# A three-operation gelu derivative, eight evictions on VectorE, and a later fill in the last chunk of a speech joint's gradients

## The chip, the core and the metric

The kernel runs on one core of a Trainium2 chip. A core has five engines that work side by side, each through its own queue of instructions in order: TensorE (PE; its weight loads are listed as PEld), VectorE (DVE), ScalarE (ACT), GpSimd (POOL) and SyncE (SP, which only issues DMAs here). The metric is the time of one execution on the device in microseconds, and the figure is the median of several runs.

## The reference

The reference is a forward pass with its gradients. Two batches of 16000 rows with 256 features go through two convolutions of three taps, each followed by the tanh form of gelu and by dropping every second row, which leaves 4000 rows. Their projection is added to that of eight prompt rows, tanh is taken of every pair, and a last product gives the output. All seven gradients are returned with it.

```python
def _fwd_reference(x, w1, w2, g, w_f, w_g, w_o):
    ...
    for i in range(K):
        h = h + jnp.einsum("btc,cd->btd", xp[:, i:i+T, :], w1[i])
    h = _gelu(h)[:, ::2, :]
    ...
    for i in range(K):
        f = f + jnp.einsum("btc,cd->btd", hp[:, i:i+T1, :], w2[i])
    f = _gelu(f)[:, ::2, :]
    fe = jnp.einsum("btd,de->bte", f, w_f)
    ge = jnp.einsum("bud,de->bue", g, w_g)
    j = jnp.tanh(fe[:, :, None, :] + ge[:, None, :, :])
    return jnp.einsum("btud,dv->btuv", j, w_o)

def reference(x, w1, w2, g, w_f, w_g, w_o, grad_out):
    ...
    _out, _vjp = jax.vjp(_f, x, w1, w2, g, w_f, w_g, w_o)
    _grads = _vjp(grad_out)
```

## The kernel before

The 2 x 4000 columns that remain lie in one row of 8016 (16 columns between the batches are padding). It is cut into 16 chunks of 512; the last has 336. An iteration n of the main loop (L865) does the joint of chunk n, four pairs of prompt rows after each other (`joint_units`, L705), and beside it, as a "fill" that `weave` (L773) deals out in steps between the joint's own steps, the forward convolutions of chunk n+1 (`conv_units`, `conv2_units`, `fe_units`) and the backward pass of chunk n-1 (`d1_units` to `e_units`). A framework fixes each engine's instruction order when the program is built. It follows the written order, its own estimate of when inputs are ready, and some orders that the kernel demands (`add_manual_dep`, `pinned`).

**Joint.** For each prompt row u, `tanh` (L423, ScalarE) writes JT and the square of it (L664, ScalarE) writes JSQ, which has two buffers. L672 (TensorE) multiplies the output gradient into a PSUM tile, and L676 (VectorE) makes NGZ of it and JSQ; there are two such tiles, mt = 0 and 1, for each u. GpSimd adds NGZ over the eight u into ACCN (L695); the last addition writes NGFE, which the backward product L460 reads. L721 (TensorE) makes the output in blocks of 128 columns, L723 (ScalarE) evicts each into OUT, and L748 stores it. L760 (TensorE) accumulates the gradient of w_o from JR, the transposed JT that SyncE fetches by a DMA transpose (L702).

**gelu.** `gelu` (L287) returns two lists of operations. The first (square, L277 product, sigmoid, second product) gives the activation. The second (L302 to L306) gives the derivative for the backward pass, with five VectorE operations. A chunk has three calls: two for the first convolution (its even and odd positions, G1) and one for the second (G2). The first lists run from a queue `later`, the second lists from a queue `late`, which is emptied in the second half of an iteration; from chunk 2 on their order is kept as written. In the profile the first list stands under L277, the line that takes it off its queue (or under L345); the second stands under L285 (the wrapper `pinned`) for chunks 2 to 15 and under L282 for chunks 0 and 1. G2 is read in L462, G1 in L486, and both multiply a PSUM tile.

**PSUM.** All products except the accumulator of L760 write to tiles of one pool of seven buffers (`psp`, L124), which are handed out in turn. Whoever asks for the eighth tile waits until the first has been emptied.

**Ends.** Iteration 0 has no backward pass; its fill starts with six empty steps. Iteration 15 has no forward pass. The fill that is left when the joint of an iteration has ended is done behind it (L899).

Of the kernel before, what the change touches and what calls it, by code (L numbers as in the profile page):

```python
# [15 lines left out]
ALU = mybir.AluOpType  # L16
# [2 lines left out]
GELU_K = 0.044715  # L19
GELU_R = float(np.sqrt(0.044715))  # L20
GELU_A = float(2.0 * np.sqrt(2.0 / np.pi))

P = 128
KT = 2
# [3 lines left out]
U = 8  # L28
CW = 512
# [3 lines left out]
def kernel(  # L33
# [250 lines left out]
    def pinned(op, n):  # L284
        return op if n <= 1 else (lambda: tc.keep_in_program_order(op()))  # L285

    def gelu(xb, W, h, gp, off, kts=((0, KT),), spare=False):  # L287

        sq, s = scratch("g_sq", spare), scratch("g_s", spare)
        TT, TS, STT = nc.vector.tensor_tensor, nc.vector.tensor_scalar, nc.vector.scalar_tensor_tensor  # L290
        first, second = [], []
        for (k0, k1) in kts:
            sq_, s_, x_ = sq[:, k0:k1, :W], s[:, k0:k1, :W], xb[:, k0:k1, :W]
            h_, gp_ = h[:, k0:k1, off:off + W], gp[:, k0:k1, off:off + W]
            first += [
                partial(nc.scalar.activation, out=sq_, in_=x_, func=ACT.Square, scale=GELU_R),
                partial(STT, out=s_, in0=sq_, scalar=1.0, in1=x_, op0=ALU.add, op1=ALU.mult),
                partial(nc.scalar.activation, out=s_, in_=s_, func=ACT.Sigmoid, scale=GELU_A),
                partial(TT, out=h_, in0=s_, in1=x_, op=ALU.mult),
            ]  # L300
            second += [
                partial(TS, out=sq_, in0=sq_, scalar1=3.0 * GELU_A, scalar2=GELU_A, op0=ALU.mult, op1=ALU.add),  # L302
                partial(TS, out=x_, in0=s_, scalar1=-1.0, scalar2=1.0, op0=ALU.mult, op1=ALU.add),
                partial(TT, out=sq_, in0=sq_, in1=x_, op=ALU.mult),
                partial(TT, out=sq_, in0=sq_, in1=h_, op=ALU.mult),
                partial(TT, out=gp_, in0=sq_, in1=s_, op=ALU.add),  # L306
            ]
        return first, second
# [2 lines left out]
    HALVES = ((0, 1), (1, 2))  # L311

    seconds0 = []

    def conv_units(n):
        c0, W = geom(n)
        seconds = []
        st = S[n]
        HT = htp.tile([P, 2, KT, CW + 2], BF16, name="HT")
        G1 = g1p.tile([P, 2, KT, CW + 2], BF16, name="G1")  # L320
        st["HT"], st["G1"] = HT, G1
        if n == G - 1:
            nc.gpsimd.memset(G1[:, 0, :, 2 + W:3 + W], 0.0)
        if n == 0:
            nc.gpsimd.memset(HT[:, 1, :, 1:2], 0.0)
            nc.gpsimd.memset(G1[:, 1, :, 1:2], 0.0)
        else:
            nc.gpsimd.tensor_copy(out=HT[:, 1, :, 1:2], in_=S[n - 1]["HT"][:, 1, :, CW + 1:CW + 2])
        taps = {0: ((1, 0, 0), (2, 1, 0), (0, 3, -1)), 1: ((0, 1, 0), (2, 3, 0), (1, 2, 0))}
        for par in range(2):  # L330
            xb = gel.tile([P, KT, CW], BF16, name="g_x")
            for mt in range(KT):
                ps = ps_f32()
                k = 0
                for (i, c, sh) in taps[par]:
                    for kt in range(KT):
                        nc.tensor.matmul(ps[:, :W], lhsT=W1[:, i, kt, mt * P:(mt + 1) * P],  # L337
                                         rhs=st["X", c][:, kt, 16 + sh:16 + sh + W], start=(k == 0), stop=(k == 5))
                        k += 1
                nc.scalar.copy(out=xb[:, mt, :W], in_=ps[:, :W])  # L340
                yield
            first, second = gelu(xb, W, HT[:, par], G1[:, par], 2, HALVES if n == 0 else ((0, KT),))
            if par == 1 and n > 1:
                for j in (1, 3):
                    first[j] = partial(lambda f: held.append(f()), first[j])  # L345
            later.extend(first)
            seconds += second
            if n == 0:
                pump(len(first))
        seconds0.extend(seconds)  # L350
        if n > 0:
            seconds0.append(lambda: nc.gpsimd.tensor_copy(out=G1[:, 1, :, 1:2],
                                                          in_=S[n - 1]["G1"][:, 1, :, CW + 1:CW + 2]))

    def conv2_units(n):
        c0, W = geom(n)
        st = S[n]
        HT = st["HT"]
        if n > 0:
            pump(len(later))  # L360
        FT = packed(ftp.tile([P, KT, CW], BF16, name="FT")[:], "k w", n, k=KT)
        G2 = ftp.tile([P, KT, CW], BF16, name="G2")
        st["FT"], st["G2"] = FT, G2
        xb = scratch("g_x", n == 0)
        for mt in range(KT):
            ps = ps_f32()
            k = 0
            for (i, par, off) in ((1, 0, 2), (0, 1, 1), (2, 1, 2)):
                for kt in range(KT):
                    nc.tensor.matmul(ps[:, :W], lhsT=W2[:, i, kt, mt * P:(mt + 1) * P],  # L370
                                     rhs=HT[:, par, kt, off:off + W], start=(k == 0), stop=(k == 5))
                    k += 1
            nc.scalar.copy(out=xb[:, mt, :W], in_=ps[:, :W])
            yield
        first, second = gelu(xb, W, FT, G2, 0, HALVES if n == 0 else ((0, KT),), n == 0)
        if n == 0:
            for f in first:
                f()
        else:
            later.extend(first)  # L380
        late.extend(pinned(f, n) for f in second + seconds0)
        seconds0.clear()
        late_open[0] = True
# [62 lines left out]
    def d1_units(n):  # L446
        c0, W = geom(n)
        st = S[n]
        GF = gfp.tile([P, KT, CW + 4], BF16, name="GF")
        st["GF"] = GF  # L450
        if n > 0:
            nc.gpsimd.tensor_copy(out=GF[:, :, 1:2], in_=S[n - 1]["GF"][:, :, CW + 1:CW + 2])
        else:
            nc.gpsimd.memset(GF[:, :, 1:2], 0.0)
        if n == G - 1:
            nc.gpsimd.memset(GF[:, :, 2 + W:3 + W], 0.0)
        for mt in range(KT):
            ps = ps_f32()
            for kt in range(KT):
                nc.tensor.matmul(ps[:, :W], lhsT=WFT[:, kt, mt * P:(mt + 1) * P], rhs=st["NGFE"][:, kt, :W],  # L460
                                 start=(kt == 0), stop=(kt == KT - 1))
            nc.vector.scalar_tensor_tensor(out=GF[:, mt, 2:2 + W], in0=st["G2"][:, mt, :W], scalar=-1.0,  # L462
                                           in1=ps[:, :W], op0=ALU.mult, op1=ALU.mult)
            yield

    def d5_units(n):
        st = S[n]
        c0, W = geom(n)
        N = W + 1 if n == G - 1 else W
        GF, G1 = st["GF"], st["G1"]  # L470
        GH = ghp.tile([P, 2, KT, CW + 4], BF16, name="GH")
        st["GH"] = GH
        if n == 0:
            nc.gpsimd.memset(GH[:, 0, :, 1:2], 0.0)
        else:
            nc.gpsimd.tensor_copy(out=GH[:, 0, :, 1:2], in_=S[n - 1]["GH"][:, 0, :, CW + 1:CW + 2])
        for par, taps in ((0, ((1, 0),)), (1, ((2, -1), (0, 0)))):
            for mt in range(KT):
                ps = ps_f32()
                k, last = 0, len(taps) * KT - 1  # L480
                for (i, sh) in taps:
                    for kt in range(KT):
                        nc.tensor.matmul(ps[:, :N], lhsT=W2T[:, i, kt, mt * P:(mt + 1) * P],  # L483
                                         rhs=GF[:, kt, 2 + sh:2 + sh + N], start=(k == 0), stop=(k == last))
                        k += 1
                gh = nc.vector.tensor_tensor(out=GH[:, par, mt, 2:2 + N], in0=ps[:, :N],  # L486
                                             in1=G1[:, par, mt, 2 - par:2 - par + N], op=ALU.mult)
                while held:
                    tc.add_manual_dep(held.pop().ins, gh.ins.name, NOSYNC, reason="held")
                yield  # L490
# [190 lines left out]
    def ngfe_acc(n, u):  # L681
# [10 lines left out]
        if u == U - 1:  # L692
            st["NGFE"] = ngp.tile([P, KT, CW], BF16, name="NGFE")
            out = st["NGFE"][:, :, :W]
        st["last"] = nc.gpsimd.tensor_tensor(out=out, in0=in0, in1=st["NGZ", u][:, :, :W], op=ALU.add)  # L695

    def load_jr(n, up):

# [6 lines left out]
    def joint_units(n, up):  # L705
# [10 lines left out]
        def o_block(k):  # L716
            o, M = bl[k]
            ps = ps_f32()
            for j, u in enumerate(us):
                for kt in range(KT):  # L720
                    nc.tensor.matmul(ps[:M, j * V:(j + 1) * V], lhsT=st["JT", u][:, kt, o:o + M], rhs=WO[:, kt, :],  # L721
                                     start=(kt == 0), stop=(kt == KT - 1))
            nc.scalar.copy(out=OUT[:M, k, :], in_=ps[:M, :])  # L723

        pend = prev_gwo[0]
        o_block(0)
# [138 lines left out]
    for n in range(G):  # L865
# [11 lines left out]
            parts.append(e)  # L877
        else:
            parts += [empty(6), islice(conv2, 1), empty(3), conv2, empty(6), fe_units(n + 1)]
        fill = chain(*parts)  # L880
        ratio = (0.92 if n > 0 else 0.4) if n + 1 < G else 0.72
        for up in range(U // 2):
# [105 lines left out]
```

## Time and profile before

| | us |
|---|---|
| median of the runs | 823.95 (820.92 to 828.51, three runs) |
| the profiled execution | 822.13 |
| its span, first to last instruction | 820.4 |
| TensorE busy | 797.0 |
| ScalarE busy | 677.1 |
| VectorE busy | 623.8 |
| GpSimd busy | 394.4 |

The profile is that of one execution. A row of the timeline gives the start in us from the span's start, the duration in us, the engine, the line of the kernel, the operation, the tiles written and read, their sizes, how many instructions the row merges and, in brackets, the engine's idle time before it and what ended it. A row in the list of waits gives who waited for whom, the total in us, how often, and the longest. TensorE's granted clock was 0.995 of full speed over the span.

### The profile page before, as it was taken

Reading aid. Unit: us, or ns where it says so; the run is one execution under the profiler, and the core shown is the slowest. Engines: PE = TensorE matmul, PEld = TensorE weight load, DVE = VectorE, ACT = ScalarE, POOL = GpSimd, SP = SyncE. Lnnn points to the kernel's source line nnn. Section 1 sums busy time; section 2 is a strip of 40 time slices with the busy share of each in tenths; the row PEclk is TensorE's granted clock in tenths of the full one; section 3 lists DMA queues with packets and bytes.
Section 4 is the critical chain, followed back from the end, with each engine's and each line's share of the span. In section 5 each row is a group of like instructions: output and inputs, shape, how many; then the busy total and the mean of one; then the engine's idle time right before and its main releaser. Section 6 shows DMA issues by size and latency. Waiting matters only on the chain.

```text
span 820.4 us, 16444 instructions
## 1 busy us (share of the span) xinstructions
PE 797.0 (97%) x6234; PEld 593.2 (72%) x6310; DVE 623.8 (76%) x1190; ACT 677.1 (83%) x1076; POOL 394.4 (48%) x419
## 2 busy tenths in 40 slices
PE   8888999999999999999999999999999999999998
PEld 3455777868678676777767778676786777778796
DVE  4995786877869778697887878868697786968634
ACT  4988997896979969799797978969799697988643
POOL 1265553553544535545476634535455345445551
PEclk9999999999999999999999999999999999999999
DMA  9989999999999999999999999999999999999944
GB/s 213 236 187 250 236 258 244 249 235 181 275 257 241 228 211 209 253 245 196 248 234 220 241 196 237 255 250 272 218 249 221 261 231 251 246 226 272 242 121 142
DMA packets 401423, 189.38 MB, mean 231 GB/s; under 512 B 349296, under 2 KB 385048, under 8 KB 401344
## 3 DMA queue, kind: packets, MB, share of 16 engines
q1 hardware_dynamic: 381104, 121.43, 80.5%
q0 software_dynamic: 20240, 66.89, 27.1%
q8 instruction: 49, 0.80, 0.5%
q14 instruction: 30, 0.25, 0.1%
HBM read 51.39 MB, written 50.34 MB: 124 GB/s over the span
## 4 chain that ended last, share of the span: by engine, by line
PE 82%; ACT 8%; DMA 4%; DVE 3%; issue 1%; SPq 1%; POOL 0%; POOLq 0%; DVEq 0%; ACTq 0%
PE GWO_ps L760 12%; PE ps L721 12%; PE ps L672 10%; PE ps L640 9%; PE ps L627 9%; PE ps L337 7%; PE ps L564 5%; PE pst L496 5%; PE ps L370 4%; PE ps L483 4%; ACT JT L423 3%; DMA JR<-JT 3%; PE ps L546 2%; PE ps L460 1%; ACT JSQ L664 1%
## 5 line engine op out<-in xcount | busy, mean ns | idle before, releaser
L695 POOL TENSOR_TENSOR ACCN<-ACCN,NGZ 128x1024 f32<-128x1024 f32 (+1 forms) x80 | 169.3, 2117 | 76.2 <-DVE NGZ L676 75.3
L676 DVE SCALAR_TENSOR_TENSOR NGZ<-JSQ,ps 128x512 bf16<-128x512 bf16 (+3 forms) x272 | 168.4, 640 | 41.0 <-PE ps L672 31.2
L723 ACT CAST OUT<-ps 128x512 bf16<-128x512 f32 (+1 forms) x252 | 145.8, 595 | 38.4 <-PE ps L721 38.3
L423 ACT ACTIVATE JT<-FE,GE 128x512 bf16<-128x512 f32 (+3 forms) x272 | 176.2, 711 | 0.5
L664 ACT ACTIVATE JSQ<-JT 128x1024 bf16<-128x1024 bf16 (+1 forms) x128 | 134.9, 1059 | 36.2 <-DVE NGZ L676 36.1
L721 PE MATMUL ps<-WO,JT 128*128 128x256 bf16 (+1 forms) x1008 | 150.6, 274 | 3.5 <-DVE NGZ L676 3.4
L760 PE MATMUL GWO_ps<-GO,JR 128*128 128x256 bf16 (+1 forms) x1008 | 149.2, 273 | 2.7 <-DMA JR<-JT 1.8
L748 POOL DMA_DIRECT2D out_dram<-OUT x76 | 55.8, 734 | 172.3 <-ACT OUT L723 156.0
L672 PE MATMUL ps<-GOT,WOT 128*128 128x512 bf16 (+1 forms) x481 | 132.6, 374 | 1.4 <-DVE W2T L845 1.0
L760 PEld LDWEIGHTS <-JR 128*128 128x128 bf16 (+1 forms) x1008 | 97.1, 98 | 29.5 <-DMA JR<-JT 3.7
L721 PEld LDWEIGHTS <-JT 128*128 128x128 bf16 (+1 forms) x1008 | 97.9, 99 | 25.8 <-issue 4.6
L627 PE MATMUL ps<-W1T,GH 128*128 128x256 bf16 (+2 forms) x756 | 100.4, 273 | 0.7
L277 DVE SCALAR_TENSOR_TENSOR g_s<-g_sq,g_x 128x1024 bf16<-128x1024 bf16 (+2 forms) x35 | 67.6, 1930 | 36.7 <-ACT g_sq L277 36.7
L627 PEld LDWEIGHTS <-GH 128*128 128x128 bf16 (+2 forms) x756 | 83.5, 116 | 13.0
L337 PE MATMUL ps<-XC,W 128*128 128x512 bf16 (+1 forms) x358 | 85.9, 377 | 1.7 <-DMA XC<-in_x_dram 1.0
L640 PE MATMUL ps<-rows,XR 128*128 128x256 bf16 (+1 forms) x708 | 84.7, 273 | 0.0
L444 DVE TENSOR_TENSOR ACC<-ACC,ps 128x512 f32<-128x512 f32 x84 | 57.5, 684 | 32.6 <-PE ps L564 26.2
L630 ACT CAST GX<-ps 128x512 bf16<-128x512 f32 (+2 forms) x126 | 72.3, 588 | 7.8 <-PE ps L627 5.2
L640 PEld LDWEIGHTS <-XR 128*128 128x128 bf16 (+1 forms) x708 | 69.3, 98 | 11.0
L259 POOL DMA_DIRECT2D out_dram<-GX x66 | 36.2, 549 | 82.8 <-ACT GX L630 81.3
L672 PEld LDWEIGHTS <-WOT 128*128 128x128 bf16 x512 | 48.2, 98 | 33.5 <-issue 2.1
L337 PEld LDWEIGHTS <-W 128*128 128x128 bf16 x384 | 37.7, 99 | 39.7 <-issue 2.1
(132 smaller groups left out, 1218.4 us busy)
## 6 DMA issues: line engine op xcount, KB each, us to landing
GO<-in_grad_out_dram SPq DMA_DIRECT2D x56, 512.0 KB, 5.7
out_dram<-OUT POOLq DMA_DIRECT2D x56, 512.0 KB, 6.0
out_dram<-GX POOLq DMA_DIRECT2D x55, 256.0 KB, 5.0
XR<-in_x_dram POOLq DMA_DIRECT2D x36, 256.0 KB, 7.8
XR<-in_x_dram POOLq DMA_DIRECT2D x12, 320.0 KB, 8.1
GO<-in_grad_out_dram SPq DMA_DIRECT2D x4, 384.0 KB, 4.9
out_dram<-OUT POOLq DMA_DIRECT2D x4, 384.0 KB, 4.4
GOT<-in_grad_out_dram SPq DMA_TRANSPOSE x68, 6.6
```

What stands on the lines that cost most here:

```text
L337: nc.tensor.matmul(ps[:, :W], lhsT=W1[:, i, kt, mt * P:(mt + 1) * P], rhs=st["X", c][:, kt, 16 + sh:16 + sh + W], start=(k == 0), stop=(k ...
L423: act = nc.scalar.activation(out=JT[:, mt, lo:hi], in_=S[n]["FE"][:, mt, lo:hi], func=ACT.Tanh, bias=GE[:, b, mt, u:u + 1], scale=1.0)
L627: nc.tensor.matmul(ps[:M, cj * D:(cj + 1) * D], lhsT=GH[:, par, kt, o:o + s * (M - 1) + 1:s], rhs=W1T[:, i, kt, :], start=(j == 0), stop=( ...
L630: nc.scalar.copy(out=t[:M, 2 * cp:2 * cp + 2, :], in_=ps[:M, :])
L640: nc.tensor.matmul(ps[:, dt * D:(dt + 1) * D], lhsT=x_row(4 * k + i + 2 * (1 - par))[:M, dt * P:(dt + 1) * P], rhs=t[:M, g + 2 * par:g + 2 ...
L664: jsq = nc.scalar.activation(out=JSQ[:, :, :W], in_=JT[:, :, :W], func=ACT.Square)
L672: nc.tensor.matmul(ps[:, :W], lhsT=WOT[:, kt, mt * P:(mt + 1) * P], rhs=GOT[:, kt, :W], start=(kt == 0), stop=(kt == KT - 1))
L676: nc.vector.scalar_tensor_tensor(out=NGZ[:, mt, lo:hi], in0=JSQ[:, mt, lo:hi], scalar=1.0, in1=ps[:, lo:hi], op0=ALU.subtract, op1=ALU.mul ...
L695: st["last"] = nc.gpsimd.tensor_tensor(out=out, in0=in0, in1=st["NGZ", u][:, :, :W], op=ALU.add)
L721: nc.tensor.matmul(ps[:M, j * V:(j + 1) * V], lhsT=st["JT", u][:, kt, o:o + M], rhs=WO[:, kt, :], start=(kt == 0), stop=(kt == KT - 1))
L723: nc.scalar.copy(out=OUT[:M, k, :], in_=ps[:M, :])
L760: nc.tensor.matmul(GWO_ps[:, dt, :], lhsT=JR[:M, j, dt, k, :], rhs=GO[:M, k, j * V:(j + 1) * V], start=(n_gwo[0] == 0), stop=(n_gwo[0] == ...
```

## The change

Three things are changed.

1. The derivative of gelu takes three operations of the form (a op scalar) op b in place of two of the form (a op scalar) op scalar and three of two tensors. The result is the derivative divided by SLOPE = -3 GELU_A; the readers multiply it back: L462 with the scalar that was -1, and L486, which becomes an operation of the form (a op scalar) op b. The copy of the column at a chunk's edge (L352) becomes a multiplication, since chunk 0 keeps the five operations and the unscaled derivative.
2. In chunk 0 the output blocks with odd k (two of four, in each of the four pairs) are evicted by VectorE in place of ScalarE.
3. In iteration 15 the fill starts with two empty steps, and the last addition of that chunk's NGZ (u = 7) is done by VectorE in place of GpSimd.

```diff
+SLOPE = -3.0 * GELU_A
...
             second += [
+                partial(STT, out=sq_, in0=sq_, scalar=1.0 / 3.0, in1=x_, op0=ALU.add, op1=ALU.mult),
+                partial(STT, out=sq_, in0=s_, scalar=1.0, in1=sq_, op0=ALU.subtract, op1=ALU.mult),
+                partial(STT, out=gp_, in0=sq_, scalar=1.0 / SLOPE, in1=s_, op0=ALU.add, op1=ALU.mult),
+            ] if scaled else [
                 partial(TS, out=sq_, in0=sq_, scalar1=3.0 * GELU_A, scalar2=GELU_A, op0=ALU.mult, op1=ALU.add),
                 partial(TS, out=x_, in0=s_, scalar1=-1.0, scalar2=1.0, op0=ALU.mult, op1=ALU.add),
                 partial(TT, out=sq_, in0=sq_, in1=x_, op=ALU.mult),
                 partial(TT, out=sq_, in0=sq_, in1=h_, op=ALU.mult),
                 partial(TT, out=gp_, in0=sq_, in1=s_, op=ALU.add),
             ]
...
+    def slope(n):
+
+        return SLOPE if n else 1.0
...
-            seconds0.append(lambda: nc.gpsimd.tensor_copy(out=G1[:, 1, :, 1:2],
-                                                          in_=S[n - 1]["G1"][:, 1, :, CW + 1:CW + 2]))
+            seconds0.append(lambda: nc.gpsimd.tensor_scalar(out=G1[:, 1, :, 1:2], in0=S[n - 1]["G1"][:, 1, :, CW + 1:CW + 2],
+                                                            scalar1=slope(n - 1) / slope(n), scalar2=None, op0=ALU.mult))
...
-            nc.vector.scalar_tensor_tensor(out=GF[:, mt, 2:2 + W], in0=st["G2"][:, mt, :W], scalar=-1.0,
+            nc.vector.scalar_tensor_tensor(out=GF[:, mt, 2:2 + W], in0=st["G2"][:, mt, :W], scalar=-slope(n),
                                            in1=ps[:, :W], op0=ALU.mult, op1=ALU.mult)
...
-                gh = nc.vector.tensor_tensor(out=GH[:, par, mt, 2:2 + N], in0=ps[:, :N],
-                                             in1=G1[:, par, mt, 2 - par:2 - par + N], op=ALU.mult)
+                gh = nc.vector.scalar_tensor_tensor(out=GH[:, par, mt, 2:2 + N], in0=G1[:, par, mt, 2 - par:2 - par + N],
+                                                    scalar=slope(n), in1=ps[:, :N], op0=ALU.mult, op1=ALU.mult)
...
-        st["last"] = nc.gpsimd.tensor_tensor(out=out, in0=in0, in1=st["NGZ", u][:, :, :W], op=ALU.add)
+        engine = nc.vector if (n, u) == (G - 1, U - 1) else nc.gpsimd
+        st["last"] = engine.tensor_tensor(out=out, in0=in0, in1=st["NGZ", u][:, :, :W], op=ALU.add)
...
-            nc.scalar.copy(out=OUT[:M, k, :], in_=ps[:M, :])
+            (nc.vector.tensor_copy if n == 0 and k % 2 else nc.scalar.copy)(out=OUT[:M, k, :], in_=ps[:M, :])
...
+        if not fwd:
+            parts.insert(0, empty(2))
         fill = chain(*parts)
```

The calls of `gelu` pass `scaled=n > 0`.

More of the change, by code (lines that the diff above doesn't have):

```diff
@@ L285, in pinned, with gelu @@
         return op if n <= 1 else (lambda: tc.keep_in_program_order(op()))
-    def gelu(xb, W, h, gp, off, kts=((0, KT),), spare=False):
+    def gelu(xb, W, h, gp, off, kts=((0, KT),), spare=False, scaled=True):
         sq, s = scratch("g_sq", spare), scratch("g_s", spare)
@@ L341, in conv_units @@
                 yield
-            first, second = gelu(xb, W, HT[:, par], G1[:, par], 2, HALVES if n == 0 else ((0, KT),))
+            first, second = gelu(xb, W, HT[:, par], G1[:, par], 2, HALVES if n == 0 else ((0, KT),), scaled=n > 0)
             if par == 1 and n > 1:
@@ L374, in conv2_units @@
             yield
-        first, second = gelu(xb, W, FT, G2, 0, HALVES if n == 0 else ((0, KT),), n == 0)
+        first, second = gelu(xb, W, FT, G2, 0, HALVES if n == 0 else ((0, KT),), n == 0, n > 0)
         if n == 0:
```

## The prediction

> **What bounds the kernel now.** I read the page's busy shares first, then who TensorE waits for, then the timeline of one chunk in the middle. The busy shares:
>
> ```profile
> PE 797.0 (97%) x6234; PEld 593.2 (72%) x6310; DVE 623.8 (76%) x1190; ACT 677.1 (83%) x1076; POOL 394.4 (48%) x419
> ```
>
> TensorE is busy for 97% of the span. The waits of TensorE over the whole span add up to little:
>
> ```profile
> PE ps L721 <- DVE NGZ L676: 3.4, 2, 2.0
> PE ps L460 <- POOL NGFE L695: 2.3, 2, 1.5
> PE ps L370 <- DVE HT L277: 2.2, 2, 2.0
> PE GWO_ps L760 <- DMA JR<-JT: 1.8, 3, 1.4
> ```
>
> Asked for 99 to 745 us alone, the same view gives a single wait of 0.4 us. From chunk 2 on TensorE streams without a gap, 49.77 us a chunk (the second forward product L370 of consecutive chunks starts at 589.12 and 638.89). So two things follow. Only the first 70 us and the hand-over to the last chunk at 761 us hold anything to gain; and in the middle every microsecond that VectorE makes TensorE wait is a microsecond of the end. The question is how far VectorE's evictions are ahead there. The timeline of VectorE, then of GpSimd and of TensorE, in one such chunk:
>
> ```profile
> 596.08 2.72 DVE L277 SCALAR_TENSOR_TENSOR g_s<-g_sq,g_x 128x1024 bf16<-128x1024 bf16 x1 [0.62 <-ACT g_sq L277]
> 598.83 0.43 DVE L285 TENSOR_SCALAR g_sq<-g_sq 128x1024 bf16<-128x1024 bf16 x1
> ...
> 601.11 0.69 DVE L285 TENSOR_TENSOR g_sq<-g_sq,g_x 128x1024 bf16<-128x1024 bf16 x1
> 601.84 0.69 DVE L285 TENSOR_TENSOR g_sq<-g_sq,FT 128x1024 bf16<-128x1024 bf16 x1
> ...
> 606.38 0.69 DVE L676 SCALAR_TENSOR_TENSOR NGZ<-JSQ,ps 128x512 bf16<-128x512 bf16 x1 [0.40 <-PE ps L672]
> 607.00 0.08 DVE L676 DVE_READ_ACCUMULATOR NGZ<-JSQ,ps 128x1 f32 x1
> 607.00 0.69 DVE L285 TENSOR_TENSOR G<-g_sq,g_s 128x1024 bf16<-128x1024 bf16 x1
> 607.60 0.68 DVE L676 SCALAR_TENSOR_TENSOR NGZ<-JSQ,ps 128x512 bf16<-128x512 bf16 x1
> ```
>
> ```profile
> 595.60 2.12 POOL L695 TENSOR_TENSOR ACCN<-ACCN,NGZ 128x1024 f32<-128x1024 f32 x1 [0.34 <-DVE NGZ L676]
> ...
> 608.44 2.19 POOL L695 TENSOR_TENSOR ACCN<-ACCN,NGZ 128x1024 f32<-128x1024 f32 x1 [0.23 <-DVE NGZ L676]
> ```
>
> ```profile
> 605.68 1.03 PE L672 MATMUL ps<-GOT,WOT 128*128 128x512 bf16 x4
> 606.54 1.91 PE L640 MATMUL ps<-rows,XR 128*128 128x256 bf16 x16
> ...
> 610.46 1.04 PE L721 MATMUL ps<-WO,JT 128*128 128x256 bf16 x8
> ```
>
> See two things. The L277 operation lasts 2.72 us because a GpSimd sum runs until 597.72. And L672 at 605.68 fills two PSUM tiles, A and B; five more follow, and with seven buffers the two L721 tiles at 610.46 and 610.90 (half of x8) take the buffers of A and B again. B is emptied from 607.60 and free 0.74 later (a TensorE wait in the first chunk ended at 50.38 on an eviction begun at 49.64): 608.34, **2.56 us ahead of its next use**. That is all the room VectorE has.
>
> **The three operations, chunks 1 to 15.** Each call loses two TENSOR_SCALAR (0.42 us) and three TENSOR_TENSOR (0.69) and gets three SCALAR_TENSOR_TENSOR of the same size. That form is in the trace, on the same tiles, with GpSimd idle:
>
> ```profile
> 31.72 1.21 DVE L277 SCALAR_TENSOR_TENSOR g_s<-g_sq,g_x 128x1024 bf16<-128x1024 bf16 x1
> 32.86 0.67 DVE L676 SCALAR_TENSOR_TENSOR NGZ<-JSQ,ps 128x512 bf16<-128x512 bf16 x1
> ```
>
> The next instruction starts 1.14 us after it. So 3 x 1.21 = 3.6 us stands against 2 x 0.42 + 3 x 0.69 = 2.9 us: fewer operations, more time. One that needs the result just before it costs 0.12 more (0.73 start to start at 601.11, 0.60 at 607.00): 1.26.
>
> The Trainium skill (VectorE: DVE Perf Modes, Rules for kernel authors) advises to minimize the count of chained VectorE operations. By that rule the edit is a saving and the sum would be 818, the second rival below; the trace does not bear it out, since the 1.21 us row is 1.75 times the 0.69 us row.
>
> Now the place. In the built order of the changed kernel VectorE has, behind the L277 operation that ends at 598.84: new operation 1.14, L444 sum 0.60, FT product 0.61, two new 1.26 + 1.14, one new 1.14, L444 0.60, two new 1.26 + 1.14, two new 1.26 + 1.14, then A. Sum 11.29, so A starts at 610.13 instead of 606.38. Then A 0.61, the ninth new operation 1.14, and B starts at 611.88, free at 612.62. The second L721 tile wants it at 610.90: **TensorE waits 1.72 us**. Everything behind it (the weight gradient L760, the next L721 and L672) queues in order and moves too. The tiles after B are freed 0.6 us apart, and TensorE takes them 0.9 to 1.3 us apart, so no second wait follows. ScalarE's square L664, which needs B's JSQ buffer back, waits until 612.6, and its evictions behind it come 1.5 us late, beside a TensorE that is 1.7 us late. No GpSimd sum falls in 598 to 612; the collisions of before (a TENSOR_SCALAR at 609.75 took 1.17 us, a product at 612.16 took 2.50) go away, but they lay behind B, where nothing waited.
>
> The 13 full iterations (n = 1 to 13) show the same times to 0.1 us apart from two whose L277 took 2.63 and 2.48; in all 13 B's room is 2.55 to 2.89 us. So 13 x 1.72 = **+22.4 us**. Iteration 14 works on the 336-column chunk; the operation takes 0.85 us at 128x672, B starts near 755.0, is free at 755.8 and wanted at 757.25: nothing. Bounds: without the 0.12 us surcharges 1.36 a chunk (17.7), and with whole durations in place of start-to-start times (9 x 0.07 more) 2.35 (30.5). The L486 product becomes SCALAR_TENSOR_TENSOR: 0.68 us (the L462 row) for 0.69, nothing. The GpSimd copies of two columns become multiplications (0.24 us each, GpSimd idle for half the span): nothing.
>
> **First chunk.** Eight of 16 evictions (0.47 us apart) leave ScalarE, 3.8 us, and join VectorE, 8 x 0.60 = 4.8 us. In the built order the HT product comes ahead of the derivative's operations, one of which took 2.34 us beside a GpSimd sum from 36.76 on; TensorE's wait of 2.0 us for HT at 39.76 goes. Tanh of the later units comes earlier on ScalarE, so the JR transposes are issued earlier (wait of 1.4 us at 67.73), and eight to ten L760 products fill the time before. What is late next is VectorE: two of its three-operation calls and the FT chain meet GpSimd sums of 2.1 to 2.4 us between 40 and 60. TensorE's waits from 36 to 70 us sum to 7.8 us in its timeline (2.0, 1.4, 0.2, 2.0, 0.8, 1.4). I take half, **-4 us**. Bounds: -8 (all go) and +2 (odd tiles held by a VectorE that a sum blocks once).
>
> **Last chunk.** L460 waited 1.49 us at 762.75 for the NGFE sum of GpSimd. With two empty units ahead, the built order puts two more L672 pairs and an L721 tile (0.28 + 0.28 + 0.44 us) before it, and GpSimd's sum moves ahead of two memsets that waited for TensorE until 760.10: **-1.5 us**, bounds 0 and -1.7. The last sum on VectorE: GpSimd ended it at 793.3, L460 reads it at 798.99, 5.7 us of cover; nothing.
>
> **Sum.** The profiled execution took 822.1 us (span 820.4). 822.1 + 22.4 - 4 - 1.5 = 839.0. The median shown, 823.95, is 1.8 above that execution; I add half: **840 us**.
>
> **Rivals.** (1) *The first chunk gives nothing* or loses 2 us, because VectorE is its bound (busy nearly without a gap from 31 to 52 us): 844 to 848. For it: the collisions there. Against: TensorE's largest wait is for an order of VectorE that goes. Chance 0.12. (2) *The wait on B does not come*, the other side: it decides at B free by 610.90. That takes new operations of 0.95 us instead of 1.14 (nine lie ahead of B), or an L277 operation that starts before the GpSimd sum and so ends 1.5 us earlier. With products' 0.60 us the nine end 5 us earlier, no wait: 822.1 - 5.5 = 817, plus 1 for the median: 818; with the early L277 13 x 0.2 remains: 820. Against: the 1.21 us row, and the sum started 0.4 us ahead of L277 in every chunk. Chance 0.10. (3) *The first chunk gives all* of its 8 us: 836 with the median's 1, and with the low bound of the wait 831. For it: most of these waits are for VectorE's order or for transposes that tanh releases, and both change. Against: the GpSimd sums stay. Chance 0.13. (4) *ScalarE makes a second wait*: its square waits for B, and its evictions behind it hold the buffer that L337 wants at 614.82 + 1.72. It decides at 2.4 us of lateness; I count 1.5. One more us a chunk: 853. Chance 0.05. The forecast, 837 to 844: 0.60.
>
> **Range and chances.** The range 829 to 848 takes in the forecast, (1) and (3), and the bounds of the sum except their far corners; (2) and (4) stay outside. About 1% is what a measurement of this kernel tells from no change: 815.7 to 832.2. Slower: forecast, (1), (4) and a part of (3), 0.80; same: the rest of (3) and most of (2), 0.15; faster: 0.05.
>
> **What would show it.** Right: a wait of the L721 tile for NGZ L676 near 1.7 us, once in each of the 13 full iterations (some 22 us in the list of waits), chunk period 51.5 us, L285 SCALAR_TENSOR_TENSOR at 1.21 to 1.34 us, GpSimd sums that no longer stretch L285. First chunk: no wait of L370 for HT. Last: none of L460 for NGFE. Wrong: a chunk period of 49.8 us, which would say that B was freed in time; or L285 rows under 1 us.

## The result, and the profile after

The changed kernel took **847.08 us** (median of six executions, 846.2 to 847.64); the kernel before, in six beside them, 822.43 us. The ratio is **1.028 (95% interval 1.024 to 1.032)**: slower by 2.8%. The profiled execution has a span of 845.6 us, 25.2 us more than that of before. Some executions of every kernel ran longer by 1.5% or more at a lower granted clock; the ratios leave them out, and the profiles of e7, e9 and e12, which are of such executions, are read only up to 370 us (e9: 120 us).

First the busy shares, from the page of the changed kernel. TensorE's busy time rose by 7 us and its share fell; VectorE, with 81 instructions fewer, is busy 3.1 us longer.

```profile
PE 804.0 (95%) x6233; PEld 594.3 (70%) x6310; DVE 626.9 (74%) x1109; ACT 675.0 (80%) x1068; POOL 395.0 (47%) x418
```

Then the list of waits of TensorE, asked for the middle of the changed kernel alone (117 to 740 us; columns: waiting engine, tile and line, what ended the wait, us in all, how often, the longest). Before, this stretch had a single wait of 0.4 us.

```profile
PE ps L731 <- DVE NGZ L685: 17.8, 25, 1.2
PE pst L505 <- ACT rows L507: 0.2, 1, 0.2
```

L731 is the former L721, L685 the former L676: it is the wait that was forecast. The stretch opens behind the first of the 26 waits; with it the list of the whole span has 18.0 us. These are idle times. Taken as the extra time from one product's start to the next, the 26 waits sum to 22.3 us. Here is one iteration: VectorE, GpSimd and TensorE of the changed kernel (columns: start, duration, engine, line, operation, tiles; in brackets the idle time ahead of it and what ended it).

```profile
617.01 2.73 DVE L278 SCALAR_TENSOR_TENSOR g_s<-g_sq,g_x 128x1024 bf16<-128x1024 bf16 x1 [0.62 <-ACT g_sq L278]
619.77 1.23 DVE L286 SCALAR_TENSOR_TENSOR g_sq<-g_sq,g_x 128x1024 bf16<-128x1024 bf16 x1
...
622.11 1.22 DVE L286 SCALAR_TENSOR_TENSOR g_sq<-g_s,g_sq 128x1024 bf16<-128x1024 bf16 x1
623.36 1.22 DVE L286 SCALAR_TENSOR_TENSOR G<-g_sq,g_s 128x1024 bf16<-128x1024 bf16 x1
...
629.88 1.23 DVE L286 SCALAR_TENSOR_TENSOR g_sq<-g_s,g_sq 128x1024 bf16<-128x1024 bf16 x1
631.02 0.68 DVE L685 SCALAR_TENSOR_TENSOR NGZ<-JSQ,ps 128x512 bf16<-128x512 bf16 x1
...
631.63 1.22 DVE L286 SCALAR_TENSOR_TENSOR G<-g_sq,g_s 128x1024 bf16<-128x1024 bf16 x1
632.77 0.68 DVE L685 SCALAR_TENSOR_TENSOR NGZ<-JSQ,ps 128x512 bf16<-128x512 bf16 x1
```

```profile
616.53 2.12 POOL L705 TENSOR_TENSOR ACCN<-ACCN,NGZ 128x1024 f32<-128x1024 f32 x1 [0.33 <-DVE NGZ L685]
...
633.61 2.13 POOL L705 TENSOR_TENSOR ACCN<-ACCN,NGZ 128x1024 f32<-128x1024 f32 x1 [4.42 <-DVE NGZ L685]
```

```profile
631.77 0.60 PE L731 MATMUL ps<-WO,JT 128*128 128x256 bf16 x4 [0.20 <-DVE NGZ L685]
633.51 0.60 PE L731 MATMUL ps<-WO,JT 128*128 128x256 bf16 x4 [1.14 <-DVE NGZ L685]
```

From the end of the L278 operation (619.77) to B's eviction (632.77) VectorE needs 13.0 us; before, from 598.83 to 607.60, it needed 8.77. That is 4.23 us later, less 2.56 us of room: 1.67. TensorE stands twice, 0.20 us idle for buffer A and 1.14 us for B, and loses 0.37 + 1.31 = **1.68 us** between starts. The chunk period, from one chunk's first product with the NGFE sum (L460, now L469) to the next, went from 49.77 to 51.44 us; in a period compared product by product, the order of TensorE's products is the same, and they fall behind at these two waits alone. No GpSimd sum falls among the new operations.

That product of chunk 1 is used below as a **marker** for the first chunk. It starts at 119.33 us before and at 125.44 after; 1.68 us of this is the first wait on A and B, so **the first chunk lost 4.4 us**, where a gain was forecast. The last chunk, from the product with NGFE of chunk 13 to the start of the last product, went from 99.2 to 98.5 us. The twelve chunks between the marker and chunk 13 took 617.4 us instead of 597.6. So 4.4 + 1.7 + 19.8 - 0.7 = 25.2 us, the whole difference of the spans.

The waits of TensorE in the first chunk, 30 to 100 us, before and then after:

```profile
PE ps L721 <- DVE NGZ L676: 3.4, 2, 2.0
PE ps L370 <- DVE HT L277: 2.0, 1, 2.0
PE GWO_ps L760 <- DMA JR<-JT: 1.8, 3, 1.4
PE ps L460 <- POOL NGFE L695: 0.8, 1, 0.8
PE ps L483 <- DVE NGZ L676: 0.5, 1, 0.5
```

```profile
PE GWO_ps L770 <- DMA JR<-JT: 7.5, 3, 3.4
PE ps L731 <- DVE GH L495: 2.9, 1, 2.9
PE ps L731 <- DVE OUT L733: 0.4, 1, 0.4
PE GWO_ps L770 <- issue: 0.2, 1, 0.2
```

The forecast was right that the wait for HT goes; those for NGZ and for NGFE are gone too, 6.7 us in all. But the waits for the JR transposes grew from 1.8 to 7.5 us and 3.5 us of others came, most of it for one late GH eviction: 9.2 us more.

### The profile page after: what moved, and what is told of

It reads as the page before. It is cut to its first block, busy times and chain, and to the rows that moved or that the text cites. A ratio compares the mean times of both kernels' runs of the same rounds, so it can differ in the third digit from the quotient of the medians.

```text
span 845.6 us, 16362 instructions
## 1 busy us (share of the span) xinstructions
PE 804.0 (95%) x6233; PEld 594.3 (70%) x6310; DVE 626.9 (74%) x1109; ACT 675.0 (80%) x1068; POOL 395.0 (47%) x418
## 4 chain that ended last, share of the span: by engine, by line
PE 79%; DVE 10%; ACT 6%; issue 3%; DMA 2%; POOL 0%; POOLq 0%; ACTq 0%; DVEq 0%
PE GWO_ps L770 12%; PE ps L731 11%; PE ps L681 9%; PE ps L636 8%; PE ps L649 8%; PE ps L346 8%; PE pst L505 5%; PE ps L573 5%; PE ps L492 4%; PE ps L379 4%; DVE G L286 2%; DVE g_sq L286 2%; DMA JR<-JT 2%; PE ps L555 2%; DVE NGZ L685 1%
## 5 line engine op out<-in xcount | busy, mean ns | idle before, releaser
L685 DVE SCALAR_TENSOR_TENSOR NGZ<-JSQ,ps 128x512 bf16<-128x512 bf16 (+3 forms) x272 | 167.4, 639 | 65.7 <-PE ps L681 53.4
L673 ACT ACTIVATE JSQ<-JT 128x1024 bf16<-128x1024 bf16 (+1 forms) x128 | 134.4, 1053 | 57.5 <-DVE NGZ L685 57.5
L432 ACT ACTIVATE JT<-FE,GE 128x512 bf16<-128x512 f32 (+3 forms) x272 | 172.2, 702 | 0.5
L731 PE MATMUL ps<-WO,JT 128*128 128x256 bf16 (+1 forms) x1008 | 151.1, 273 | 21.6 <-DVE NGZ L685 18.0
L733 ACT CAST OUT<-ps 128x512 bf16<-128x512 f32 (+1 forms) x244 | 140.9, 590 | 34.3 <-PE ps L731 32.1
L731 PEld LDWEIGHTS <-JT 128*128 128x128 bf16 (+1 forms) x1008 | 97.4, 98 | 48.3 <-issue 25.5
L278 DVE SCALAR_TENSOR_TENSOR g_s<-g_sq,g_x 128x1024 bf16<-128x1024 bf16 (+2 forms) x35 | 68.3, 1951 | 33.1 <-ACT g_sq L278 33.1
```

The costliest lines, as they stand in the source:

```text
L432: act = nc.scalar.activation(out=JT[:, mt, lo:hi], in_=S[n]["FE"][:, mt, lo:hi], func=ACT.Tanh, bias=GE[:, b, mt, u:u + 1], scale=1.0)
L673: jsq = nc.scalar.activation(out=JSQ[:, :, :W], in_=JT[:, :, :W], func=ACT.Square)
L685: nc.vector.scalar_tensor_tensor(out=NGZ[:, mt, lo:hi], in0=JSQ[:, mt, lo:hi], scalar=1.0, in1=ps[:, lo:hi], op0=ALU.subtract, op1=ALU.mul ...
L733: (nc.vector.tensor_copy if n == 0 and k % 2 else nc.scalar.copy)(out=OUT[:M, k, :], in_=ps[:M, :])
```

## The experiments

In all of them but e10 the kernel before is the base; e10 starts from the changed kernel. "Marker" is net of 1.7 us wherever the waits on A and B precede it. Ratios are to the kernel before on the same chip. The edits are shown in short; `...` marks what is left out, and STT is the operation of the form (a op scalar) op b.

### The three parts, one at a time

**e1, the derivative alone:**

```
 second += [
+    STT sq = (sq + 1/3) * x
+    STT sq = (s - 1) * sq
+    STT gp = (sq + 1/SLOPE) * s
+] if scaled else [          # scaled = n > 0
...
+SLOPE in L462, L486 and in the edge columns of G1
```

> The three-operation derivative alone (chunks 1 to 15, with its multiplied edge columns and slopes); evictions, fill and last sum as before. Theory: the thirteen waits on the VectorE eviction of PSUM buffer B make the loss, 13 x 1.68 us in the trace of the changed kernel = +21.9 us, and the 4.3 us that its first chunk lost are the evictions': 822.4 + 21.9 = 844 us (842.5 to 846). Rival: the first chunk's loss comes from the three longer operations of chunk 1's calls, which run there beside GpSimd sums: 822.4 + 21.9 + 4.3 = 848 to 849 us.

Measured: 845.57 us, ratio 1.033 (1.024 to 1.041). The 26 waits sum to 22.5 us between starts: they are there in full without the other parts. The median lies in the theory's range, though the interval takes in both expectations; the marker, 120.8, puts the first chunk's loss at 1.4 us, neither none nor 4.3.

**e4, the same from chunk 2 on:**

```
-scaled = n > 0
+scaled = n > 1
```

> The three-operation derivative from chunk 2 on; chunk 1, whose derivative runs in the first chunk's iteration, keeps five operations. Theory: the thirteen full iterations lose 1.68 us each and nothing else changes: 822.4 + 21.9 = 844 us (843 to 846), chunk period 51.45 us, start of the first wait within 0.5 us of the kernel before's time for that product. Rival: the loss of a chunk depends on how far the first chunk has set the engines back, so that it is under 1.2 us here: below 838 us.

Measured: ratio 1.028 (1.019 to 1.037, from two runs of 843.02 and 848.79 us; the first is the profiled one), chunk period 51.45 us. TensorE's waits in the thirteen iterations (100 to 745 us):

```profile
PE ps L734 <- DVE NGZ L689: 18.2, 26, 1.2
PE pst L509 <- ACT rows L511: 0.2, 1, 0.2
```

The same 26 waits, 22.5 us between starts, now behind a first chunk that kept its five operations. So the loss of a chunk does not depend on how the first chunk went, and the rival falls. The marker, 118.3, is 1.1 us earlier than before, more than the 0.5 us expected; the section on the first chunk shows that one and the same first chunk differs by more than this between executions.

**e2, the evictions alone:**

```
-nc.scalar.copy(out=OUT[:M, k, :], in_=ps[:M, :])
+(nc.vector.tensor_copy if n == 0 and k % 2 else nc.scalar.copy)(out=OUT[:M, k, :], in_=ps[:M, :])
```

> Only the first chunk's odd output evictions on VectorE. Theory: they are what the first chunk lost in the changed kernel, 4.3 us (an output store that is issued late because GpSimd is in a sum when the VectorE eviction ends, ScalarE waiting for that buffer, its tanh and the transposes of JR behind it late): 826 to 827 us, the loss before 112 us. Rival: they cost nothing by themselves, or gain up to the 4 us of the prediction: 818 to 822.5 us.

Measured: ratio 1.000 (0.997 to 1.004), marker 119.3. The theory (they lose 4.3 us, a ratio of 1.005) falls: alone they lose no such amount, and a gain cannot be seen either; the interval leaves room for some 3 us both ways. Their waits, 30 to 100 us:

```profile
PE GWO_ps L760 <- DMA JR<-JT: 7.1, 2, 4.9
PE ps L337 <- DVE NGZ L676: 2.1, 2, 1.5
PE ps L483 <- DVE NGZ L676: 0.9, 1, 0.9
PE ps L483 <- DVE GF L462: 0.8, 1, 0.8
```

As in the changed kernel, the waits for HT and at L721 are gone and JR is waited for instead.

**e3, the last chunk alone:**

```
+engine = nc.vector if (n, u) == (G - 1, U - 1) else nc.gpsimd
+st["last"] = engine.tensor_tensor(...)
...
+if not fwd:
+    parts.insert(0, empty(2))
```

> Only the last chunk: two empty units ahead of the fill, and the last sum on VectorE. Theory: the wait of the second-last product for the NGFE sum falls from 1.66 to 0.66 us, as in the trace of the changed kernel: 822.4 - 1.0 = 821.4 us, a ratio of 0.9988. Rival: the empty units only move the wait to another place, 0.0 us: 822.4; or all of the wait goes: 820.8.

Measured: ratio 0.9985 (0.995 to 1.002), too small to tell from nothing by the time alone. In the traces, 715 us to the end, the wait for NGFE is 1.5 us before and 0.7 us here:

```profile
PE ps L460 <- POOL NGFE L696: 0.7, 1, 0.7
```

From the product with NGFE of chunk 13 to the start of the last product it took 98.4 us, 0.8 less than before, near the 1.0 of the theory. The wait does not go entirely.

### Is it VectorE's added time, or what stands ahead of B?

**e5 and e6** put the three-operation form into one call of the three (G2), and into two (G2 and the first G1), from chunk 2 on:

```
+SCALED = ("G2",)          # e6: ("G2", 0)
+def slope(n, call):
+    return SLOPE if n > 1 and call in SCALED else 1.0
```

> From chunk 2 on the three-operation form in one call of the three a chunk has (G2 alone); the two G1 calls keep five operations. Theory (a wait only beyond the 2.56 us by which PSUM buffer B was free ahead of its next use): B's eviction starts 0.6 us later than before, less than 2.56: no wait, 822.4 us (820.5 to 824), chunk period 49.8 us. Rival (VectorE's added time reaches the end in proportion): a third of 1.68 us a chunk, 822.4 + 13 x 0.56 = 829.7 us, period 50.3.

> From chunk 2 on the three-operation form in two calls of the three (G2 and the first G1 call). Theory: B's eviction starts 2.7 us later than before, 0.2 us more than the room: 822.4 + 13 x 0.2 = 825 us (822.4 to 828.5 for a wait of 0 to 0.45 us), period 49.8 to 50.2 us. Rival (in proportion): two thirds of 1.68 us a chunk, 822.4 + 14.6 = 837 us, period 50.9.

Measured, e5: no interval for the ratio, but a profiled execution of 822.71 and a lowest of 819.65 us (the kernel before's lowest on that chip 818.86), chunk period 49.77 us: TensorE waits nowhere in a regular chunk, and the proportional rival with its 50.3 falls. (Behind the marker the whole trace is 2.4 us longer than that of before, at the seventh and eleventh period and in the last two chunks; the rival's sum was 7.3.) e6: ratio 1.010 (1.004 to 1.016), chunk period 50.55 us, where 49.8 to 50.2 was expected. B was late by as much as expected: the two L733 tiles of one iteration

```profile
261.24 1.20 PE L733 MATMUL ps<-WO,JT 128*128 128x256 bf16 x8
```

took 1.20 us for eight products, where eight L721 products without a wait took 1.04; the trace puts the wait down to DVE NGZ, and 0.17 us it is (0.2 expected). But the period grew by 0.78. Another 0.6 us a chunk goes between 228 and 232 us, at products that wait for ScalarE's evictions and VectorE's NGZ. ScalarE has there a square (L676) ahead of the g_x eviction, which came first before, and starts g_sq some 1.6 us later. That this order makes the 0.6 us was only read from the trace. So with one, two and three calls B's eviction began 0.58, 2.73 and 4.23 us later behind the L278 operation than before, and the waits on A and B cost 0, 0.17 and 1.68 us a chunk: what exceeds the room of 2.56 us, not a proportion.

**e7 and e12** keep all nine operations, and let them in more slowly in the full iterations:

```
 def weave(main, fill, ratio, slow=False):
...
-        pump_late(1)
+        pump_late(0 if slow and step % 2 else 1)          # e12: step % 3 == 1
...
+weave(main, fill, ratio, 0 < n < G - 2)
```

> From chunk 2 on the three-operation form in all three calls, but in the full iterations one of these operations is let in at every second step of the main loop, where it was one at each step. Five of the nine then stand ahead of B's eviction and four behind. Theory (only what stands ahead of B's eviction counts): B is evicted before its next use, no wait: 822.4 us (821 to 825), period 49.8 us, with VectorE as busy as in the changed kernel. Rival (the longer form costs TensorE time wherever it stands): 844 us, period 51.45; or the operations now pile up behind and hold a later eviction: 826 to 835.

> From chunk 2 on the three-operation form in all three calls, and in the full iterations one of these operations at two of every three steps of the main loop. Seven of the nine stand ahead of B's eviction (nine in the changed kernel, five at half pace), and the last two lie between other evictions rather than three in a row at the iteration's end. Theory: two operations of 1.2 us fewer ahead of B put its eviction 4.23 - 2.4 = 1.8 us later than before, less than the 2.56 us of room: no wait on B, nor the small ones at the iteration's end that half pace had; period 49.8 us, 822 us (820.5 to 824). Rival (half pace lost because the longer form has a price of its own wherever it stands): period 50.15 or more, 827 us and above.

Measured, e7: ratio 1.010 (1.006 to 1.015), chunk period 50.16 us. The waits on A and B are gone, but 0.23 + 0.18 us are lost at the iteration's end, where three of the operations, one of them stretched to 3.04 us by a GpSimd sum, now stand in a row ahead of two NGZ evictions: part of the theory, part of the second rival. e12: ratio 1.006 (1.000 to 1.011), chunk period 49.77 us, exactly that of before; up to 370 us TensorE has no wait of 0.1 us or more behind the first chunk. The product with NGFE of two consecutive chunks:

```profile
316.70 0.59 PE L472 MATMUL ps<-NGFE,WFT 128*128 128x512 bf16 x2
...
366.47 0.59 PE L472 MATMUL ps<-NGFE,WFT 128*128 128x512 bf16 x2
```

The same nine operations, of 1.22 us where no GpSimd sum meets them, cost a chunk 1.67 us where nine stand ahead of B, 0.4 with five ahead and three in a row behind, nothing with seven ahead. So the form has no price of its own in TensorE's time in these chunks. e12's whole time is still some half a per cent above that of before, with an interval that reaches 1.000. Why, its trace, up to 370 us, does not tell.

### The first chunk

In e2 and after, JR is what TensorE waits for. SP's queue in e2 shows why it is late: behind the gradient rows GO.

```profile
36.66 1.97 SPq L174 DMA_TRANSPOSE GOT<-in_grad_out_dram  x1
38.68 0.58 SPq L204 DMA_DIRECT2D GO<-in_grad_out_dram  x1
39.35 5.61 SPq L702 DMA_TRANSPOSE JR<-JT  x1
```

So in **e8** (before), **e10** (after) and **e11** (before with the evictions and the last chunk's part, five operations throughout) GO was put behind JR in chunk 0:

```
-nc.sync.dma_start(out=t[p0:p1, k:k + nb, :], in_=joint_dram(grad_out, b, q, m, up, nb))
+dma = nc.sync.dma_start(...)
+if n == 0 and up > 1:
+    tc.add_manual_dep(dma.ins, S[0]["JRD", up - 1].ins.name, NOSYNC, reason="rows behind tanh rows")
```

and in **e9** (evictions alone) chunk 0's weight gradient did not wait for JR at all; it multiplies the constant WO, so the true share of chunk 0 in the gradient of w_o is left out:

```
-lhsT=JR[:M, j, dt, k, :]
+lhsT=JR[:M, j, dt, k, :] if n else WO[:M, dt, 0:P]
```

> The kernel before with one change of order: in chunk 0 the loads of the gradient rows GO of the third and fourth pair of units are queued behind the JR transposes of the pair before, where they stood ahead of them. Marker: start of the product with the NGFE sum (L460) of chunk 1, 119.3 us in the kernel before. Theory (in the first chunk the JR transposes come last): its three waits for JR, 2.3 us in sum, shrink: marker 117 to 118.5, 820 to 822 us. Rival: those waits are hidden or only move to GO: marker 119 to 120, 822.4 us.

> The first chunk's odd evictions on VectorE, and the weight gradient L760 of chunk 0 reads the constant WO where it read JR; the JR transposes are still made, but nothing waits for them (left out: chunk 0's true share of that gradient). Theory: the evictions do take away 3.5 to 5 us of waits for VectorE, as the prediction had it, and the waits for JR, 7.4 us in the run with the evictions alone, take their place; without them the marker (L460 of chunk 1) falls from 119.3 to 112 to 116 us and the time to 815 to 819. Rival: the evictions have no gain of their own: marker 118 to 119.5, 821 to 822.5 us.

> The changed kernel with GO behind JR in chunk 0, as in the run of the kernel before with that order. Its marker is 125.4 us (119.3 before; 1.7 of the 6.1 between them are the first wait on buffer B). Theory (JR, 8.0 us of waits, is what its first chunk lost): marker 121.5 to 123.5, 843 to 845 us. Rival (the 16 DMA engines are full there, so GO comes late instead): marker 125 to 126, 847 us.

> The kernel before with five operations throughout, the first chunk's odd evictions on VectorE, the last chunk's two empty units and last sum on VectorE, and GO behind JR in chunk 0. Theory (JR holds the gain of the evictions): marker 115.5 to 118 instead of 119.3, last chunk 0.9 us shorter: 817.5 to 819.5 us, a ratio of 0.994 to 0.9965. Rival (GO late instead of JR): 821.5 us, 0.999.

Measured: e8 ratio 0.999 (0.995 to 1.004), marker 121.0, waits for JR 2.5 us: nothing gained. e9 ratio 1.005 (1.001 to 1.009), marker 117.9: short of the theory's 112 to 116, because 3.7 us of waits for VectorE's own OUT evictions came up, 1.9 us for NGFE, and a JR wait of 2.3 us in chunk 1. Its SP queue has another order than that of e2 too (JR at 37.71 us ahead of GO at 40.04), so it does not change one thing alone. e10 845.29 us, ratio 1.025 (1.017 to 1.033), marker 121.3: 2.5 us earlier than in the changed kernel, as far as expected, but not for the reason given: its JR waits hardly shrank (7.1 us, 5.7 of it in one). e11 **ratio 0.9955 (0.9911 to 0.9999)**, marker 115.7, profiled execution 818.19 us: faster than both kernels, by an interval that only just excludes no change. There SP's queue reads:

```profile
35.46 1.87 SPq L174 DMA_TRANSPOSE GOT<-in_grad_out_dram  x1
37.42 2.20 SPq L705 DMA_TRANSPOSE JR<-JT  x1
39.68 0.79 SPq L204 DMA_DIRECT2D GO<-in_grad_out_dram  x1
```

JR is issued 1.9 us earlier, in 2.20 us instead of 5.61, and the L763 products run at 43.08 without a wait; in e2 they started at 48.84, after 4.89 us of it.

By waits alone these markers make no sense: e8 and e11 differ by 5.3 us, their waits between 30 and 100 us only by 1.6 (9.7 against 8.1 in their lists). What is missing is the granted clock. Stretches of 4 us of the changed kernel (columns: window, length, then busy us and instructions of TensorE, weight loads, VectorE, ScalarE, GpSimd; last three: **granted clock**, DMA share, GB/s):

```profile
44.00:48.00 4.00, 1.26 (x7) 0.87 (x7) 4.00 (x8) 1.94 (x4) 2.26 (x3) 0.65 1.25 219
48.00:52.00 4.00, 4.00 (x14) 1.91 (x13) 1.17 (x3) 0.95 (x2) 3.75 (x2) 0.50 1.17 209
60.00:64.00 4.00, 1.57 (x6) 0.99 (x8) 4.00 (x8) 0.55 (x1) 2.53 (x2) 0.78 1.09 240
64.00:68.00 4.00, 4.00 (x19) 1.86 (x17) 4.00 (x4) 3.60 (x7) 4.00 (x4) 0.79 0.93 238
```

and TensorE around the first of them:

```profile
46.74 1.89 PE L770 MATMUL GWO_ps<-GO,JR 128*128 128x256 bf16 x8 [3.38 <-DMA JR<-JT]
48.42 2.76 PE L379 MATMUL ps<-HT,W 128*128 128x512 bf16 x6
```

Behind the 3.38 us wait the products run at half the clock: six L379 products take 2.76 us, and 1.46 at 38.17 us, at full clock. So a wait can be paid for a second time. Summing (1 - granted clock) x 4 us over such windows from 16 to 116 us gives the time withheld:

| run | marker, net (us) | withheld (us) | rest (us) |
|---|---|---|---|
| before | 119.3 | 3.4 | 115.9 |
| changed kernel | 123.8 | 6.8 | 117.0 |
| e1, derivative | 120.8 | 3.4 | 117.4 |
| e4, derivative from chunk 2 (first chunk as before) | 118.3 | 3.4 | 114.9 |
| e2, evictions | 119.3 | 1.7 | 117.6 |
| e3, last chunk (first chunk as before) | 119.6 | 3.4 | 116.2 |
| e5, one call (first chunk as before) | 117.3 | 0.0 | 117.3 |
| e6, two calls (first chunk as before) | 117.6 | 1.7 | 115.9 |
| e7, half pace (first chunk as before) | 117.5 | 1.7 | 115.8 |
| e8, before, GO behind | 121.0 | 5.2 | 115.8 |
| e9, JR not waited for | 117.9 | 1.7 | 116.2 |
| e10, after, GO behind | 121.3 | 5.1 | 116.2 |
| e11, evictions, GO behind | 115.7 | 0.0 | 115.7 |
| e12 (first chunk as before) | 117.6 | 0.0 | 117.6 |

The withheld time comes in lumps of 1.7 us, and it makes most of the spread: beside the profiled execution of before, the changed kernel's first chunk lost 3.4 of its 4.4 us to two more lumps, and e11 gained 3.4 of its 3.6 by having none. A lump that falls into a wait costs nothing there: in the changed kernel the half clock began at 45.21 us, 1.5 us before the long wait ended. Over TensorE's busy time alone 5.9 us were withheld against 3.2, so 2.7 of the 4.4 us; its idle time grew by 2.4 us.

The number of lumps is not fixed by the kernel. In the six runs marked "first chunk as before" every engine has the operations up to 97 us in the order of the kernel before. With that kernel these are seven executions of one first chunk, and they took 117.3 to 119.6 us, with no lump, one or two. The rest, 114.9 to 117.6 among these seven, is as wide as in the whole table, so no part of the change can be read from it. A difference of one or two lumps between two traces, as between e2, e8, e9 and before, shows nothing by itself. The mean granted clock is on record for every run, though, to 0.001, and times the span it gives what was withheld in the whole run. In the six runs of the changed kernel that is 5.1 to 7.6 us, 6.3 in the mean; in the 57 runs of before that stand beside the experiments, on four chips, 0 to 7.5, 3.1 in the mean. So the loss of granted clock comes with the change, some 3 us on average, and varies with the execution. In nine runs of e11 it is 2.0 in the mean, beside 3.8 for before on the same chip: 1.8 us gained, not the 3.4 of the one trace.

One other loss of the changed kernel is plain. Its 2.9 us wait for GH at 83 us is a product of VectorE that a GpSimd sum met:

```profile
82.27 3.29 DVE L354 TENSOR_TENSOR HT<-g_s,g_x 128x1024 bf16<-128x1024 bf16 x1 [0.24 <-ACT g_s L278]
85.48 0.68 DVE L495 SCALAR_TENSOR_TENSOR GH<-G,ps 128x512 bf16<-128x512 bf16 x1
```

```profile
82.87 2.13 POOL L705 TENSOR_TENSOR ACCN<-ACCN,NGZ 128x1024 f32<-128x1024 f32 x1
```

The HT product takes 0.69 us alone (e2 has it at 79.39, ahead of the sum). Here it lasts until the sum is done, the GH eviction stands behind it, and TensorE behind that. In e10 the same wait of 2.9 us came up again, in e1 and e2 not. Removing this one meeting was not tried.

## Why the prediction was right in its main term and wrong in a part

Slower was right, and the main term was right by its mechanism. The time was not: 847.08 us lies outside the 837 to 844 of the forecast, and 0.9 us inside the end of the range. It is there by luck in part: the first chunk lost 4.4 us, more than its worst bound of 2, and 0.9 us less lost in the chunks behind, with the 1 us added for the median, kept the sum inside.

**The derivative, +22.4 us: right.** Measured 1.68 us a chunk against 1.72, thirteen times, 21.5 us by the markers and 22.3 by the waits. The steps hold one by one: operations of 1.22 us (L286; forecast 1.21 to 1.34); a chunk period of 51.44 us (51.5); A from VectorE 11.25 us behind L278 (11.29) and B 13.00 (13.04). One detail was off: the forecast put the wait on B alone, but A was late too, by 0.37 us, as its own figures say (A begun at 610.13 is free 0.74 later, at 610.87, and was wanted at 610.46); the sum is the same, since TensorE's lateness at A counts toward B. e5, e6 and e12 show the reason given, B's place against its next use, to be the cause. The rule of the Trainium skill that was weighed (VectorE: DVE Perf Modes, Rules for kernel authors: keep the count of chained operations low; the row also advises against fusing for speed) would have given a saving; nine operations in place of fifteen made the kernel slower, because each took 1.22 us instead of 0.42 or 0.69 and all nine stood ahead of B.

**ScalarE's second wait (rival 4): rightly kept low.** Its squares wait 57.5 us for NGZ instead of 36.1, and no second wait of TensorE followed in after, e1 or e4. e6 has small ones of that kind, 0.6 us a chunk.

**The first chunk, -4 us: wrong in sign.** The step that failed is "I take half" of the waits from 36 to 70 us. That VectorE's waits go was right: HT's, and NGZ's with it. The first rival, with no gain or a loss of 2 us, was nearer, and its 844 to 848 us hold the result, though its own terms (822.1 + 22.4 - 1.5 + 1, and 2 more) reach only 846. Its reason, VectorE as the bound, fits 3.3 of the 11 us of waits (GH and OUT); the larger part is another. Two things were missing. The JR transposes were taken to come earlier with tanh; they are queued on SP behind GOT and GO, and TensorE, no longer held at HT, reached their products before they had landed. And a long wait of TensorE was priced at its own length, where the trace shows up to 1.7 us more for each lump of half clock: the three long waits of the changed kernel (3.38, 3.40, 2.86 us) were followed by two, one and one.

**The last chunk, -1.5 us: right in kind, too large.** The wait for NGFE fell from 1.49 to 0.50 us of idle time, 0.7 us by the last chunk's length and 0.8 in e3. The forecast took it to vanish. The last sum on VectorE cost nothing that can be seen.

**The sum.** 822.1 + 21.5 + 4.4 - 0.7 = 847.3, beside 840 forecast; the difference is the first chunk's term, 8.4 us off, less 0.9 us on the derivative, plus 0.8 on the last chunk, less the 1 us added for the median.

## What to carry to other kernels

Count the time that an edit puts ahead of each eviction, and compare it with the room that eviction has before its buffer is used again: here a delay below the room cost nothing, and above it every microsecond counted in every iteration. Fewer operations are no gain by themselves: nine in place of fifteen lost 1.68 us a chunk, and the same nine with two of them moved behind the eviction lost none. When a stall is removed, look at the queue that delivers what is used next, its order included, before booking the stall as a gain. In a stretch with stalls, read the granted clock next to the waits, and more than one execution of it before putting a few microseconds down to an edit.

## What was not expected of the hardware

The granted clock of TensorE falls to half behind long waits, and that takes up to 1.7 or 3.4 us: around the end of the wait of 3.38 us and behind it the clock was 0.65 and 0.50 in two windows of 4 us. All seven waits above 2.8 us in the first chunks of after, e1, e2 and e10 were followed by such a stretch. Shorter ones were sometimes: in the kernel before, the clock was 0.57 from 40 to 44 us behind a wait of 1.99 us, and 1.00 behind one of 2.03 us at 57 us. The fourteen traces, as far as they are read here, show what decides. The clock changes only at steps of 3.41 us, counted within a trace from its first record, and half clock follows a step in which TensorE, by its listed products, was idle for about 2 us. Of the steps at full clock all 13 with over 2.07 us idle were followed by half clock, of the seven with 1.85 to 2.07 four, and of those with less none. So it matters how a wait falls on the steps, and short waits add up: half clock came at 67.37 us in the kernel before, behind one step with 0.85 us of one wait and 1.0 us of the next. The Trainium skill (TensorE: Matmul & The Clock Gate, Part 1) speaks of a free-running activity window of about 3.4 us after which an idle TensorE gets half its clock. The lumps of 1.7 us, half of 3.4, agree with that length; that 2 us of idle time in the 3.4 are enough is what the traces add.

The issue of one JR transpose held SP for 5.61 us right behind a GO load and for 2.20 us ahead of it, with a tile of the same size; that GO is the cause was not tried apart from the order. Over the whole of e2 the 64 issues took 1.5 to 7.8 us.
